# Two empty steps between the transfer of the roots and the products with it, and steps that begin with chunk 0 in the first layer

## The chip, the cores and the metric

The kernel runs on one core of a Trainium2 chip. The metric is the device time of one execution in microseconds (us); the number for a kernel is the median of several runs. The profile comes from one more execution with the hardware profiler on.

## What is computed

Causal block attention over 4 batches of 8 heads, then two feed-forward layers over the 2304 tokens. The first layer multiplies two products; the second normalises its input by the root of the mean square, gates with a sigmoid and multiplies. Cut to what matters here:

```python
x = attention(q, k, v)                 # (2304, 512), blocks of 64 masked causally
a, b = x @ w_a, x @ w_b                # d_model 512, d_ff 1536
x = (a * b) @ w_out                    # the first layer's output
rms = np.sqrt(np.mean(x * x, axis=-1, keepdims=True) + 1e-06)
xn = x / rms * rms_g                   # the step that is edited
g = xn @ w_gate
val = xn @ w_val
out = (g * (1 / (1 + np.exp(-g))) * val) @ w_out2
```

## The kernel before, in words

The tokens run along the free dimension, so an activation tile has 128 partitions of features and up to 768 columns of tokens. Every matrix product is made of three matmuls, with operands split into a high and a low part (names that begin with h and l; `split` at L99 and L109 makes them, the high part on ScalarE).

The first layer runs over five blocks of tokens (512, 256, 512, 512, 512), the second over three blocks of 768, each in two halves of 384. A block goes through d_ff in chunks: 12 chunks in the first layer (`moe1`), 24 in the second (`moe2`), where a chunk is half of the work for one of the two weight matrices over a pair of d_ff tiles. Between chunks lie the output products (`output`, L438 to L440), whose sums VectorE adds into `acc` (L447). Attention and the preparation of the weights for the second layer run beside the first layer.

In the second layer a product by blocks needs seven matrix products per weight matrix. Their sums are formed on VectorE out of PSUM: `u` (L528) from a copy p of the first product and the second, then `p` (L539) and a second `u` (L545), then c (L547, L550, L554), then the gate: `asb` (L561) or `g` (L566), and the split hh, hl of g. TensorE has six PSUM banks for this, so a bank is free for the next product only when VectorE has read it.

Normalisation of the next block is done while the current block is worked on. `normed` is a generator: each `next` runs it to its next `yield`, which is called a step here. Its steps are: squares of the four feature groups and their sum on ScalarE and VectorE (L688 to L691) and the split of the sum into sh and sl (steps 1 and 2); the sum over partitions on TensorE with a matrix of ones (L702, L703, tile r), and a transfer of the row of means to DRAM (step 3); a transfer that spreads it over 128 partitions of 6 numbers (step 4); the root and its reciprocal on 128 x 6 numbers and a transfer back (L710 to L716, step 5); and the transfer that spreads the row of roots over all partitions, into y (L718, step 6). Then come four products of x with the weights of the norm and y (L722, one per step), four differences T of halves of x (L642, one per step), and one step that hands them over. For the first block of the second layer seven more steps split these operands; for later blocks that is done with the last output products.

The steps are called in `before_fc`, before each chunk: two per chunk in the last block of the first layer (of 12 chunks), one per chunk in the second layer (of 24 chunks), from chunk 1 on in both.

```python
            if fc >= 1:
                for _ in range(FC * 2 // n_tiles):
                    got["x"] = next(norm, None) or got.get("x")
```

Which instruction stands where on an engine is not the program's order alone: a scheduler places the instructions of each engine by their priority, which follows the place where they are emitted, and by its own estimate of when their inputs are ready. `behind(ins, "gate")` adds that an instruction stands behind the latest g. All transfers are issued on SyncE's queue, in order: weights (L230, L234, L238), blocks of weights to be prepared (L162), outputs, and the small rows of the steps.

Of the kernel before, what the change touches and what calls it, by code (L numbers as in the profile page):

```python
# [45 lines left out]
def tile_attention_moe_moe(  # L46
# [57 lines left out]
    def split(hi, lo, src, eng_hi, eng_lo, late=None):  # L104

        ins = copy(eng_hi, hi, src)
        if eng_hi is act and late is not None:
            behind(ins, late)
        eng_lo.tensor_tensor(lo, src, hi.bitcast(F32), ALU.subtract)  # L109
        return ins  # L110
# [5 lines left out]
    def behind(ins, what):  # L116

        if what in gate:
            tc.add_manual_dep(ins.ins, gate[what].ins.name, ORDER, reason="keep behind")
# [116 lines left out]
    def fetch_o(layer, i):  # L236
        t = wtiles["o", i] = wop.tile([P, 2, TF * DM], F32R, tag="o", name="o")
        sp.dma_start(out=t.bitcast(F32), in_=wo_dram[layer][i])  # L238
# [392 lines left out]
    def sums_of(x):  # L631


        n = x.shape[2] // 2
        b = {f"B{k + 1}{m + 1}": x[:, 2 * k:2 * k + 2, m * n:m * n + n] for k in range(2) for m in range(2)}
        for e, name, p, q, tag in (
            (dve, "T1", "B12", "B11", "sq"), (dve, "T3", "B22", "B12", "t"),
            (dve, "T2", "B22", "T1", "y"), (dve, "T4", "T2", "B21", "sl"),
        ):
            t = rms["sb"].tile([P, 2 * n], F32, tag=tag, name=name)  # L640
            b[name] = t.rearrange("p (c n) -> p c n", c=2)
            behind(e.tensor_tensor(b[name], b[p], b[q], ALU.subtract), "gate")  # L642
            yield None
        yield b

    def split_sums(b, res):

        for name, el in (
            ("B11", dve), ("T2", dve), ("B21", dve), ("T1", dve), ("T3", pool), ("B22", dve), ("T4", pool),
        ):  # L650
            res[name] = [rms["sb"].tile(list(b[name].shape), F32R, tag=k + name, name=k + name) for k in "hl"]
            split(*res[name], b[name], act, el, "hh")
            yield None
# [27 lines left out]
    def normed(t0, n, parts):  # L681

        xr, ps_r = rms["sb"], rms["ps"]
        x = xr.tile([P, KC, BMAX[1]], F32, tag="xf", name="xf")[:, :, 0:n]
        sp.dma_start(out=x, in_=x2_dram[:, :, t0:t0 + n])
        sq = xr.tile([P, BMAX[1]], F32, tag="sq", name="sq")[:, 0:n]
        y = xr.tile([P, BMAX[1]], F32, tag="y", name="y")[:, 0:n]
        behind(act.activation(sq, x[:, 0, :], AF.Square), "hh")  # L688
        for c in range(1, KC):
            act.activation(y, x[:, c, :], AF.Square)  # L690
            dve.tensor_tensor(sq, sq, y, ALU.add)  # L691
            if c == 2:
                yield None
        sh = xr.tile([P, BMAX[1]], F32R, tag="sh", name="sh")[:, 0:n]
        sl = xr.tile([P, BMAX[1]], F32R, tag="sl", name="sl")[:, 0:n]
        split(sh, sl, sq, act, dve, "hh")
        yield None

        row, small = dram.tile([2, n], F32, name="row"), xr.tile([P, 3, n // P], F32, tag="sm", name="sm")
        for o, w in parts:  # L700
            ps = ps_r.tile([P, 512], F32, tag="r", name="r")
            pe.matmul(ps[:, 0:w], rms["ones"], sh[:, o:o + w], start=True, stop=False)  # L702
            pe.matmul(ps[:, 0:w], rms["ones"], sl[:, o:o + w], start=False, stop=True)  # L703
            dve.tensor_scalar(sq[0:1, o:o + w], ps[0:1, 0:w], 1.0 / DM, 1e-6, ALU.mult, ALU.add)
        sp.dma_start(out=row[0:1, :], in_=sq[0:1, :])
        v, r, t = (small[:, x, :] for x in range(3))
        yield None
        behind(sp.dma_start(out=v, in_=row[0, :].rearrange("(p n) -> p n", p=P)), "gate")
        yield None
        behind(act.activation(r, v, AF.Sqrt), "hh")  # L710
        dve.reciprocal(r, r)
        dve.tensor_tensor(t, r, r, ALU.mult)
        dve.tensor_tensor(t, t, v, ALU.mult)
        dve.tensor_scalar(t, t, -0.5, 1.5, ALU.mult, ALU.add)
        dve.tensor_tensor(r, r, t, ALU.mult)
        sp.dma_start(out=row[1, :].rearrange("(p n) -> p n", p=P), in_=r)  # L716
        yield None
        behind(sp.dma_start(out=y, in_=row[1, :].partition_broadcast(P)), "gate")  # L718
        yield None
        for c in range(KC):  # L720
            behind(
                dve.scalar_tensor_tensor(x[:, c, :], x[:, c, :], rms_g[:, c:c + 1], y, ALU.mult, ALU.mult),  # L722
                "gate",
            )
            yield None
        for b in sums_of(x):
            yield b
        if t0 == blocks[NB_FIRST][1]:

            res = {}  # L730
            for _ in split_sums(b, res):
                yield res
# [4 lines left out]
    for at, (layer, t0, n_tok, parts) in enumerate(blocks):  # L737
        following = blocks[at + 1] if at + 1 < len(blocks) else None
        with_attention = at + 1 < NB
        if layer == 1 and blocks[at - 1][0] == 0:  # L740
# [4 lines left out]
            accs = ctx.enter_context(tc.tile_pool(name="acc2", bufs=1))  # L745
        acc = accs.tile([P, KC, BMAX[layer]], F32, tag="acc", name="acc")
        norm = normed(*following[1:]) if following and following[0] == 1 else iter(())
        got = {}

# [7 lines left out]
        def before_fc(fc, n_tiles=n_tiles, at=at, layer=layer, following=following, norm=norm, got=got):  # L757
            if at == 0:
                if fc > 0:
                    for _ in range(TF):  # L760
                        if prepared[0] < len(w_pieces) // 2:
                            prepare()
            else:
                if layer == 1 and fc in (0, 4, 12, 20):
                    fetch_o(layer, (0, 4, 12, 20).index(fc))
                if layer == 0 and fc % TF == 0:
                    fetch_o(layer, fc // TF)
                if layer == 1 and rings and fc == 0 and blocks[at - 1][0] == 0:
                    for i in range(2, 6):
                        fetch_ab(layer, i)  # L770
                ahead = 2 if layer == 0 else 6
                if fc + ahead < n_tiles:
                    fetch_ab(layer, fc + ahead)
                if layer == 0:
                    n = sum(BACKGROUND[:at]) + min(BACKGROUND[at], BACKGROUND[at] * (fc + 1) // (FC - 3))
                    while prepared[0] < len(w_pieces) // 2 + n:
                        prepare()
            ahead = 2 if layer == 0 else 6
            if following and fc + ahead >= n_tiles:
                fetch_ab(following[0], fc + ahead - n_tiles)  # L780
            if fc >= 1:
                for _ in range(FC * 2 // n_tiles):
                    got["x"] = next(norm, None) or got.get("x")

# [99 lines left out]
```

## Time and profile before

| | |
|---|---|
| median of 3 runs | 1134.62 us (1134.28 to 1134.89) |
| profiled execution, its own time | 1126.49 us |
| its span, first to last instruction | 1124.7 us |
| TensorE (PE) busy | 1076.7 us, 96% |
| VectorE (DVE) busy | 748.1 us, 67% |
| ScalarE (ACT) busy | 523.6 us, 47% |
| GpSimd (POOL) busy | 466.9 us, 42% |
| mean granted TensorE clock | 0.989 |

A time is read against the profiled execution when it comes from the trace. An engine's busy share tells how much of the span it worked; what a wait costs is read where TensorE stands still.

### The profile page before, as it was taken

To read this page: it belongs to the slowest core of one execution; us is meant where nothing else is said; L and a number is where in the kernel's file an instruction comes from. 1 tells how busy PE (TensorE), PEld (TensorE's weight loads), DVE (VectorE), ACT (ScalarE), POOL (GpSimd) and SP (SyncE) were. 2 spreads that over 40 slices of the span, in tenths; PEclk is the share of its full clock that TensorE was granted. 3 is DMA by queue.
4 is the path that set the end of the run, shared out by engine and by line. 5 is a ranking of instruction groups with operands and counts; after the bars stand their busy time and mean duration, and the time that the engine had idled before them with its cause. 6 is when DMAs were issued, how large, how long until landed. Compare 5 with 4: busy or idle time off the path is not lost.

```text
span 1124.7 us, 16248 instructions
## 1 busy us (share of the span) xinstructions
PE 1076.7 (96%) x5780; PEld 956.7 (85%) x5780; DVE 748.1 (67%) x1379; ACT 523.6 (47%) x1142; POOL 466.9 (42%) x460
## 2 busy tenths in 40 slices
PE   6889989999999999899999999989999899999998
PEld 4667768689888788688887878989999899999998
DVE  5988887856876867534547483775677746765564
ACT  6877876746666765424433433431233322223120
POOL 5676677543555765335535443311222211222120
PEclk9999999999999999999999999999999999999999
DMA  5544877877887867969987889845757556475521
GB/s 176 187 155 146 276 249 253 269 268 274 296 301 260 265 245 281 327 238 374 351 316 275 315 328 379 330 165 187 253 213 281 204 187 242 175 267 196 190 82 57
DMA packets 74279, 276.48 MB, mean 246 GB/s; under 512 B 25683, under 2 KB 33363, under 8 KB 56278
## 3 DMA queue, kind: packets, MB, share of 16 engines
q1 hardware_dynamic: 74198, 275.44, 68.7%
q8 instruction: 46, 0.75, 0.3%
q14 instruction: 35, 0.29, 0.1%
HBM read 218.77 MB, written 56.64 MB: 245 GB/s over the span
## 4 chain that ended last, share of the span: by engine, by line
PE 66%; DMA 11%; DVE 10%; POOL 5%; ACT 4%; issue 3%; SPq 0%; POOLq 0%; ACTq 0%; DVEq 0%
PE mm L438 7%; PE mm L439 7%; PE mm L440 7%; PE mm L506 6%; PE mm L508 6%; PE mm L507 6%; PE mm L476 6%; PE mm L478 6%; PE mm L477 6%; PE s L312 3%; DMA st<-in_w_ab_dram 3%; DMA st<-in_w_o_dram 2%; DMA ab<-wc 2%; PE t L373 2%; PE t L347 2%
## 5 line engine op out<-in xcount | busy, mean ns | idle before, releaser
L438 PE MATMUL mm<-hh,o 128*128 128x384 f32 (+2 forms) x528 | 189.7, 363 | 8.0 <-DVE u L528 3.8
L439 PE MATMUL mm<-hh,o 128*128 128x384 f32 (+2 forms) x528 | 187.9, 357 | 0.0
L476 PE MATMUL mm<-xh,ab 128*128 128x512 f32 (+1 forms) x480 | 181.8, 382 | 2.5 <-DVE acc L447 1.1
L477 PE MATMUL mm<-xl,ab 128*128 128x512 f32 (+1 forms) x480 | 181.7, 379 | 0.0
L440 PE MATMUL mm<-hl,o 128*128 128x384 f32 (+2 forms) x528 | 181.1, 355 | 0.0
L478 PE MATMUL mm<-xh,ab 128*128 128x512 f32 (+1 forms) x480 | 180.1, 376 | 0.0
L109 POOL TENSOR_TENSOR hl<-g,hh 128x384 fp32r<-128x384 f32 (+2 forms) x76 | 87.1, 1146 | 157.9 <-ACT hh L99 156.9
L99 ACT ACTIVATE hh<-g 128x384 fp32r<-128x384 f32 (+2 forms) x132 | 70.7, 552 | 143.2 <-DVE g L566 84.1
L561 POOL TENSOR_TENSOR asb<-c,sig 128x384 f32<-128x384 f32 x36 | 37.4, 1038 | 222.4 <-ACT sig L559 222.4
L336 POOL TENSOR_SCALAR pp<-pp,st 128x64 f32<-128x64 f32 (+3 forms) x144 | 87.6, 624 | 76.9 <-DVE st L333 45.3
L438 PEld LDWEIGHTS mm<-hh,o 128*128 128x128 f32 x528 | 100.4, 190 | 19.9 <-DVE u L528 4.1
L312 PE MATMUL s<-ks,qz 128*128 128x384 f32 (+4 forms) x284 | 97.9, 434 | 11.2 <-ACT pp L321 11.0
L439 PEld LDWEIGHTS mm<-hh,o 128*128 128x128 f32 x528 | 100.6, 191 | 8.8 <-issue 1.6
L476 PEld LDWEIGHTS mm<-xh,ab 128*128 128x128 f32 x480 | 91.0, 190 | 19.6 <-DVE acc L447 1.7
L440 PEld LDWEIGHTS mm<-hl,o 128*128 128x128 f32 x528 | 99.9, 190 | 8.6 <-DVE hl L109 0.5
L447 DVE SCALAR_TENSOR_TENSOR acc<-mm,acc 128x384 f32<-128x384 f32 (+2 forms) x132 | 74.3, 587 | 46.7 <-PE mm L440 46.0
L477 PEld LDWEIGHTS mm<-xl,ab 128*128 128x128 f32 x480 | 90.7, 189 | 16.3 <-issue 0.7
L478 PEld LDWEIGHTS mm<-xh,ab 128*128 128x128 f32 x480 | 90.6, 189 | 16.3 <-issue 0.7
L506 PE MATMUL mm<-hT,ab 128*128 128x384 f32 x288 | 97.1, 338 | 2.8 <-DVE u L528 1.9
L507 PE MATMUL mm<-lT,ab 128*128 128x384 f32 x288 | 97.0, 337 | 0.0
L508 PE MATMUL mm<-hT,ab 128*128 128x384 f32 x288 | 95.0, 337 | 0.0
L321 ACT ACTIVATE pp<-s,st 128x288 f32<-128x288 f32 (+8 forms) x142 | 71.4, 505 | 40.3 <-DVE st L315 36.9
(128 smaller groups left out, 2342.3 us busy)
## 6 DMA issues: line engine op xcount, KB each, us to landing
ab<-wab SPq DMA_DIRECT2D x48, 1024.0 KB, 7.0
o<-wo SPq DMA_DIRECT2D x28, 1536.0 KB, 7.4
ab<-wc SPq DMA_DIRECT2D x36, 1024.0 KB, 7.3
ab<-wc SPq DMA_DIRECT2D x36, 768.0 KB, 4.5
st<-in_w_ab_dram SPq DMA_DIRECT2D x48, 512.0 KB, 4.1
wc<-bg SPq DMA_DIRECT2D x12, 1792.0 KB, 7.1
wab<-ab SPq DMA_DIRECT2D x12, 1024.0 KB, 5.1
st<-in_w_o_dram SPq DMA_DIRECT2D x24, 512.0 KB, 4.5
```

Source lines behind the costliest of these rows:

```text
L109: eng_lo.tensor_tensor(lo, src, hi.bitcast(F32), ALU.subtract)
L312: pe.matmul(ps[:, 0:z - a], qz[m % 2][:, b], ks[m][:, a:z], start=True, stop=True)
L336: pool.tensor_scalar(t, t, s[:, 10 + y:11 + y], 1.0, ALU.mult, ALU.mult)
L438: pe.matmul(ps[:, 0:n], wh, hh, start=(y == 0), stop=False)
L439: pe.matmul(ps[:, 0:n], wl, hh, start=False, stop=False)
L440: pe.matmul(ps[:, 0:n], wh, hl, start=False, stop=(y == TF - 1))
L476: pe.matmul(ps[:, 0:n], wh[:, a:z], xhc, start=(c == 0), stop=False)
L477: pe.matmul(ps[:, 0:n], wh[:, a:z], xlc, start=False, stop=False)
L478: pe.matmul(ps[:, 0:n], wl[:, a:z], xhc, start=False, stop=(c == KC - 1))
L506: pe.matmul(ps[:, 0:n], wh, xh[:, c, :], start=(c == 0), stop=False)
L507: pe.matmul(ps[:, 0:n], wh, xl[:, c, :], start=False, stop=False)
L508: pe.matmul(ps[:, 0:n], wl, xh[:, c, :], start=False, stop=(c == 1))
```

## The change

The transfer of the roots keeps its step 6. Two empty steps, 7 and 8, come behind it, so that the four products are steps 9 to 12 and not 7 to 10, and all later steps come two later. In the first layer the steps begin with chunk 0 instead of chunk 1 (`layer` is 0 there): steps 1 to 6 come one chunk earlier, the products come in chunks 4 and 5 as before, and 24 steps are called where 22 were. In the second layer the steps still begin with chunk 1, steps 1 to 6 stay, and products and differences come two chunks later.

```diff
@@ -716,7 +716,8 @@
         sp.dma_start(out=row[1, :].rearrange("(p n) -> p n", p=P), in_=r)
         yield None
         behind(sp.dma_start(out=y, in_=row[1, :].partition_broadcast(P)), "gate")
-        yield None
+        for _ in range(3):
+            yield None
         for c in range(KC):
             behind(
                 dve.scalar_tensor_tensor(x[:, c, :], x[:, c, :], rms_g[:, c:c + 1], y, ALU.mult, ALU.mult),
@@ -778,7 +779,7 @@
             ahead = 2 if layer == 0 else 6
             if following and fc + ahead >= n_tiles:
                 fetch_ab(following[0], fc + ahead - n_tiles)
-            if fc >= 1:
+            if fc >= layer:
                 for _ in range(FC * 2 // n_tiles):
                     got["x"] = next(norm, None) or got.get("x")
```

No instruction is added or removed. Three places in the order of the engines follow. A number behind a name is a buffer's; it differs between the two programs for the same thing. The products are at L722 before and at L723 after, one line lower.

VectorE in the second layer's first block, before (xf are the products, u, p and c the sums out of PSUM, asb and g the gate, T a difference):

```order
L561 TENSOR_TENSOR asb_7459<-c_7433,sig 128x384
L722 SCALAR_TENSOR_TENSOR xf<-xf,rms_g,y 128x768 x4
L528 TENSOR_TENSOR u_7488<-p_7479,mm 128x384
L642 TENSOR_TENSOR T_7507<-xf 128x768
L566 SCALAR_TENSOR_TENSOR g<-mm,asb_7455 128x384
L539 TENSOR_TENSOR p_7503<-u_7488,mm 128x384
L545 TENSOR_TENSOR u_7516<-u_7488,mm 128x384
```

and now:

```order
L561 TENSOR_TENSOR asb_7457<-c_7431,sig 128x384
L723 SCALAR_TENSOR_TENSOR xf<-xf,rms_g,y 128x768 x2
L528 TENSOR_TENSOR u_7486<-p_7477,mm 128x384
L723 SCALAR_TENSOR_TENSOR xf<-xf,rms_g,y 128x768
L539 TENSOR_TENSOR p_7501<-u_7486,mm 128x384
L545 TENSOR_TENSOR u_7513<-u_7486,mm 128x384
L566 SCALAR_TENSOR_TENSOR g<-mm,asb_7453 128x384
```

The first product still follows the same asb; two of the four products now stand behind the first u, the fourth further back behind the g's, and T with it.

VectorE in the second layer's second block, before:

```order
L566 SCALAR_TENSOR_TENSOR g<-c_8797,asb_8739 128x384
L722 SCALAR_TENSOR_TENSOR xf<-xf,rms_g,y 128x768
L109 TENSOR_TENSOR hl<-g,hh 128x384
L566 SCALAR_TENSOR_TENSOR g<-c_8806,asb_8743 128x384
L566 SCALAR_TENSOR_TENSOR g<-c_8815,asb_8747 128x384
L722 SCALAR_TENSOR_TENSOR xf<-xf,rms_g,y 128x768 x3
L528 TENSOR_TENSOR u_8856<-p_8847,mm 128x384
L109 TENSOR_TENSOR hl<-g,hh 128x384
L642 TENSOR_TENSOR T_8959<-xf 128x768
L539 TENSOR_TENSOR p_8871<-u_8856,mm 128x384
L545 TENSOR_TENSOR u_8883<-u_8856,mm 128x384
```

and now:

```order
L566 SCALAR_TENSOR_TENSOR g<-c_8796,asb_8739 128x384
L109 TENSOR_TENSOR hl<-g,hh 128x384
L566 SCALAR_TENSOR_TENSOR g<-c_8805,asb_8743 128x384
L566 SCALAR_TENSOR_TENSOR g<-c_8814,asb_8747 128x384
L723 SCALAR_TENSOR_TENSOR xf<-xf,rms_g,y 128x768 x3
L109 TENSOR_TENSOR hl<-g,hh 128x384
L528 TENSOR_TENSOR u_8854<-p_8845,mm 128x384
L539 TENSOR_TENSOR p_8869<-u_8854,mm 128x384
L545 TENSOR_TENSOR u_8881<-u_8854,mm 128x384
```

The first product left its place in front of hl and two g; three products stand behind these, the fourth and T behind the next chunk's g.

TensorE in the first layer's last block, before (r is the sum over partitions of sh and sl; L438 to L440 are the output products of the first three chunks):

```order
L438 MATMUL mm<-hh,o 128x512
L439 MATMUL mm<-hh,o 128x512
L440 MATMUL mm<-hl,o 128x512 x2
L702 MATMUL r<-sh,ones_r 128x384 x2
L440 MATMUL mm<-hl,o 128x512 x2
L438 MATMUL mm<-hh,o 128x512
L703 MATMUL r<-sl,ones_r 128x384 x2
```

and now (L476 to L478 are the products of the second chunk; 36 matmuls of the block lie ahead of the first r):

```order
L476 MATMUL mm<-xh,ab 128x512
L477 MATMUL mm<-xl,ab 128x512
L478 MATMUL mm<-xh,ab 128x512
L702 MATMUL r<-sh,ones_r 128x384 x2
L476 MATMUL mm<-xh,ab 128x512
L477 MATMUL mm<-xl,ab 128x512
L478 MATMUL mm<-xh,ab 128x512
L703 MATMUL r<-sl,ones_r 128x384 x2
```

The sum over partitions moved from the first output products to the middle of the second chunk. On ScalarE the squares and the split sh moved with it: the block's first decoding step `a` (L137) stood in front of the squares and now stands between them and sh. On SyncE's queue the four small transfers of the steps (L705, L708, L716, L718) moved ahead by about one weight load each in this block; in the second layer they stand where they stood.

## Rows read from the trace of the kernel before

**Rows 1.** The page, part 1: busy time, share of the span and instructions of each engine.

```profile
PE 1076.7 (96%) x5780; PEld 956.7 (85%) x5780; DVE 748.1 (67%) x1379; ACT 523.6 (47%) x1142; POOL 466.9 (42%) x460
```

**Rows 2.** Waits of TensorE, 560 to 1125 us: waited for, total us, times, longest.

```profile
PE mm L438 <- DVE u L528: 3.8, 1, 3.8
PE mm L506 <- DVE u L528: 1.9, 1, 1.9
PE mm L506 <- DVE u L545: 0.9, 1, 0.9
PE mm L506 <- DMA ab<-wc: 0.8, 1, 0.8
PE mm L476 <- DVE acc L447: 0.7, 1, 0.7
PE mm L438 <- ACT hh L99: 0.4, 1, 0.4
```

**Rows 3.** Chain that ended last, 735 to 752 us: start, us, what.

```profile
735.45 5.53 DMA y<-row
...
746.35 0.32 PE mm L438
...
750.64 0.17 PE mm L439
```

**Rows 4.** VectorE in order, second layer's first block: start, us, what, idle before.

```profile
741.00 3.98 DVE L722 SCALAR_TENSOR_TENSOR xf<-xf,rms_g,y 128x768 f32<-128x768 f32 x4 [2.99 <-DMA y<-row]
744.91 0.54 DVE L528 TENSOR_TENSOR u<-p,mm 128x384 f32<-128x384 f32 x1
745.38 0.94 DVE L642 TENSOR_TENSOR T<-xf 128x768 f32<-128x768 f32 x1
```

**Rows 5.** The same view of VectorE, second layer's second block.

```profile
873.49 1.02 DVE L722 SCALAR_TENSOR_TENSOR xf<-xf,rms_g,y 128x768 f32<-128x768 f32 x1 [1.25 <-DMA y<-row]
874.43 0.55 DVE L109 TENSOR_TENSOR hl<-g,hh 128x384 fp32r<-128x384 f32 x1
...
875.83 3.64 DVE L722 SCALAR_TENSOR_TENSOR xf<-xf,rms_g,y 128x768 f32<-128x768 f32 x3
879.39 0.54 DVE L528 TENSOR_TENSOR u<-p,mm 128x384 f32<-128x384 f32 x1
```

**Rows 6.** The same view of VectorE, first layer's last block.

```profile
647.45 3.80 DVE L722 SCALAR_TENSOR_TENSOR xf<-xf,rms_g,y 128x768 f32<-128x768 f32 x4 [3.18 <-DMA y<-row]
```

**Rows 7.** Stretches: length, busy us of each engine (instructions), granted clock, DMA, GB/s.

```profile
746.20:749.50 3.30, 3.30 (x12) 3.30 (x11) 3.30 (x8) 1.01 (x2) 1.01 (x1) 0.50 0.27 112
882.70:886.00 3.30, 3.30 (x12) 3.30 (x12) 1.91 (x4) 0.52 (x1) 0.00 (x0) 0.50 0.30 127
298.40:300.10 1.70, 0.00 (x0) 0.00 (x0) 1.63 (x4) 0.46 (x1) 1.30 (x3) 1.00 0.90 333
300.20:303.70 3.50, 3.15 (x25) 2.96 (x26) 1.96 (x7) 0.91 (x5) 0.56 (x1) 1.00 1.13 247
164.50:166.20 1.70, 0.00 (x0) 0.00 (x0) 1.46 (x3) 1.32 (x4) 0.29 (x1) 0.90 1.21 199
166.00:172.60 6.60, 6.33 (x15) 4.96 (x16) 6.43 (x15) 4.28 (x12) 4.05 (x4) 0.50 0.93 328
```

**Rows 8.** The roots' transfer, line L718, three times: from issue to landing.

```profile
DMA to landing us min/median/max: 3.6/5.5/7.4
```

**Rows 9.** ScalarE and TensorE in order, start of the first layer's last block.

```profile
599.63 0.67 ACT L137 ACTIVATE a<-st 128x512 f32<-128x512 f32 x1 [9.34 <-DMA st<-in_w_o_dram]
...
594.67 0.39 PE L476 MATMUL mm<-xh,ab 128*128 128x512 f32 x1
...
602.83 0.39 PE L476 MATMUL mm<-xh,ab 128*128 128x512 f32 x1
```

**Rows 10.** The page, part 6: weight loads of the first layer, KB, us to landing.

```profile
ab<-wab SPq DMA_DIRECT2D x48, 1024.0 KB, 7.0
```

**Rows 11.** Transfers of weights to be prepared, line L162: from issue to landing.

```profile
DMA to landing us min/median/max: 3.3/4.2/9.0
```

## The prediction

> **What bounds the kernel now.** I read the page first: TensorE is busy for 96% of the span [rows 1], so the time is TensorE's time, and only three things can move it: its amount of work, the stops in which it stands still, and the stretches in which its clock is halved. The diff adds no work to it. The second view is the list of what TensorE waited for from 560 us on, where both edited places lie [rows 2]. That list is short: 8.5 us in six stops of 0.4 us or more, and three of them, 3.8, 1.9 and 0.9 us, end with a VectorE addition of the second layer (u, lines 528 and 545). The other three are 0.8 (a weight transfer), 0.7 (VectorE's accumulation, L447) and 0.4 us.
>
> Why is u late? The chain and VectorE's own order of time show it. In the second layer's first block the transfer that spreads the row of roots takes 5.53 us [rows 3]. VectorE stands 2.99 us for it, then does the four products of L722 in a row in 3.98 us, and only then u, at 744.91 [rows 4]. TensorE has by then run out of free PSUM banks. That is the 3.8 us stop. In the next block VectorE waits 1.25 us, does one product, three short instructions, then three products from 875.83, and u starts at 879.39 [rows 5]: the stops of 1.9 and 0.9. In the first layer's last block the wait is 3.18 us [rows 6], and the accumulations queued behind the products come late: the stop of 0.7.
>
> The third view is the granted clock. After each of the two places one stretch runs at 0.50, that is 1.2 GHz instead of 2.4: in 3.30 us TensorE starts 12 matmuls there [rows 7]. The chain gives the price: one matmul per 0.32 us against 0.17 [rows 3]. About 11 matmuls fall into such a stretch, so it costs 11 x 0.15 = 1.6 us.
>
> **The second layer's first block.** The transfers stand where they stood in SyncE's queue, so I let the row land at the same 741.0. What the changed order moves are the products: two of the four now stand behind u, one of them between u and the next addition p, where the difference T (0.94 us in [rows 4]) stood before, and the fourth behind the gating products g. u comes two products earlier, 3.98 / 2 = 2.0 us, and the stop shrinks from 3.8 to 1.8 us. The order from u to p keeps its length, one operation of about 1 us in between, so I expect no new stop behind it (at most 0.4 us, since p, u and g come in another order). The differences T are late next; they are needed only at the block's end, and cost nothing as long as VectorE has the output products of TensorE to hide behind.
>
> Does the clock still fall? The trace has two stops of nearly this length, both with TensorE at 0.00 busy over 1.7 us: after the one at 164.5 the clock is 0.50, after the one at 298.4 it stays at 1.00 [rows 7]. That is even; I take the fall to stay, since the stop has the length of one that was followed by it. Gain here: 2.0 us, with 3.6 as the other end.
>
> **The second layer's second block.** Here all four products are moved behind a short VectorE chain that used to stand behind the first product. Before: wait to 873.49, one product, then hl and two g (874.43 to 875.83, 1.4 us), three products (3.64 us), u at 879.39. After: hl and the two g run inside the wait, which began at 873.49 - 1.25 = 872.24; with about 0.6 us for ScalarE's hh ahead of them (hl of the same shape takes 0.55) they end near 872.2 + 0.6 + 1.4 = 874.2. The row is there by then, so VectorE waits for nothing; three products of the same 3.64 us end near 877.9, one more hl (0.5) follows, and u starts at 878.4, so 1.0 us earlier. The stop of 1.9 becomes 0.9. Behind u no T of 0.94 us stands any more: p and the second u follow directly, 0.9 us earlier still, while TensorE has six matmuls to do (6 x 0.17 = 1.0 us). That removes the stop of 0.9. Together 2.8 becomes 0.9: gain 1.9. Stops of 0.7 and 0.8 us in [rows 2] lie in stretches that kept their clock, so I take this fall to vanish: 1.6 more, 3.5 in all. Its ends: if the row takes as long as the slowest of the three (7.4 against 3.6 us in [rows 8]), it lands at 877.3, 3 us after VectorE asks, the stop is 3.8 instead of 2.8 and the clock falls: a loss of 1.0.
>
> Against counting a clock gain while a stop remains stands one rule. The rows first: the stops of 0.7 and 0.8 us were followed by no fall. The Trainium skill, "TensorE: Matmul & The Clock Gate", section "A second HAM failure mode: psum-queue depth-cycling", says that short idles between groups of matmuls, from cycling through PSUM banks, are enough to make the clock go back and forth. By that rule the 0.9 us stop would still cost the fall, and the sum would be 1.6 us smaller; the rows on the two shorter stops speak against it here.
>
> **The first layer's last block.** The first six steps come one chunk earlier (two steps per chunk), two are empty, and the products keep chunk 4. The row of roots is therefore issued about one chunk earlier, and a chunk is 24 matmuls. 36 of them take from the block's start at 594.67 to 602.83 [rows 9], so a chunk is 5.4 us: more than the 3.18 us that VectorE waited. The wait goes, the products no longer delay L447, and the 0.7 us stop goes. The stop of 0.4 waits for ScalarE, on which the early steps' squares lie; these move too, so it may go or come back elsewhere. I count 0.7, between 0 and 1.1. On SyncE's queue four small transfers of these steps are now ahead of weight loads. Each may hold the queue until its source is ready, which costs nothing while the weights come in time: they are fetched two chunks ahead, 10.8 us, land in 7.0 us [rows 10], and no stop in [rows 2] names them. Without that cover each us of delay is a us of stop.
>
> **The sum.** 2.0 + 3.5 + 0.7 = 6.2 us. The profiled execution took 1126.49 us, and would take 1120.3. The median of the runs is 8.1 us above it; I carry the difference over unchanged: 1134.62 - 6.2 = 1128.4 us.
>
> **The rivals.**
> - *The clock stays up at both places*: the first block's 1.8 us stop behaves like the one at 298.4, and 6.2 + 1.6 = 7.8 us go: 1126.8. The two rows are even, but it also needs the second block's fall to vanish. 0.25.
> - *The clock falls at both places*: the banks are still full when u comes in the second block, TensorE idles 0.9 us, and some 11 matmuls after it run at 0.32 us each. 6.2 - 1.6 = 4.6 us, 1130.0. Against it stand the two shorter stops without a fall. 0.12. (The rule of "TensorE: Matmul & The Clock Gate" in the Trainium skill, above, would give this one.)
> - *The wait is the row, not the place*: in the second block the row lands as late as the slowest. 2.0 - 1.0 + 0.7 = 1.7 us, 1132.9. The three landings differ by a factor of two [rows 8], so it can be. 0.08.
> - *The change hardly does what it says*: the empty steps move no wait, since the scheduler, not the step, places the products, and in the first block it still puts the first one where VectorE stood 2.99 us. If the second block's products were bound the same way, 2.0 us would be all: 1132.6. The new order there speaks against it. 0.09.
> - *Slower*: in the first layer the two sum products on TensorE (r, L702 and L703) now stand in the first two chunks, and TensorE executes in order. Their operand sh stands on ScalarE behind a decoding step a that waited 9.34 us for a weight transfer, until 599.63 [rows 9]. From there 0.67 us for a and about 0.94 us each for sh and sl (an estimate, from T of the same 768 columns in [rows 4]) give 602.2; TensorE asks for sh at 602.83 and for sl about 1 us later, 603.9. So there is 1.7 us of room. Past that each us stops TensorE, with a fall of the clock on top. With the slowest such transfer, 9.0 against 4.2 us median [rows 11], 4.8 us longer: a stop of 3.1 plus 1.6 leaves 0.8 of the 5.5 us of the other layer. It turns slower by over 0.2% from a landing about 8 us later: 1134.62 - 5.5 + 6.3 + 1.6 = 1137.0. No transfer in the trace was that late. 0.06.
>
> **How the numbers follow.** The forecast itself has 0.40. About 0.2% (2.3 us) is what a measurement of this kernel can tell from no change. Forecast and the first two rivals are faster by more than that: 0.40 + 0.25 + 0.12 = 0.77. The third and fourth, 1.7 and 2.0 us, are within it: 0.17. The last is slower: 0.06. The range goes from 1125.7, which is the best case with the first layer's other 0.4 us and some tenths of spread between runs (0.6 us in the three shown), to 1133.0, which takes in both cases within 0.2%; it leaves out the slower case and the tails, under 0.2.
>
> **What would show it.** Right: TensorE's stop for u in the second layer's first block near 1.8 us, in the second below 1; one half-clock stretch from 700 us on, not two; no wait for the row in the first layer and 1 us or less in the second block, still about 3 us in the first; T behind the next g. Wrong: a wait of VectorE for the row as long as before in the second block; a stop of TensorE at r in the first layer; a stop with a weight load as its end; or stops that shrink as said while the time stays, which would mean that TensorE's pace, and not its stops, sets the end.

## The result, and the profile after

| | before | after |
|---|---|---|
| median | 1134.45 us (1132.15 to 1134.89, 4 runs) | 1119.42 us (1117.65 to 1121.29, 4 runs) |
| ratio after to before | | 0.9878, 95% interval 0.9856 to 0.9901 |
| profiled execution | 1126.49 us | 1118.77 us |
| mean granted clock | 0.989 | 0.992 |

The change makes the kernel faster by 1.2%, 15.0 us in these runs, where 6.2 were forecast. The sign was right; the time lies 6.3 us under the range.

The page of the kernel after, part 1, against [rows 1]: VectorE, ScalarE and GpSimd do the same work, and TensorE's 5780 matmuls take 4.8 us less.

```profile
PE 1071.9 (96%) x5780; PEld 954.7 (85%) x5780; DVE 750.6 (67%) x1379; ACT 523.3 (47%) x1142; POOL 465.6 (42%) x460
```

The waits of TensorE in the kernel after, 560 to 1125 us (the view of [rows 2]: waited for, total us, times, longest). Of the six stops two are left. All three of the first layer and of the border between the layers are gone, of which the prediction had counted one.

```profile
PE mm L438 <- DVE u L528: 2.0, 1, 2.0
PE mm L506 <- DVE u L528: 1.2, 1, 1.2
```

VectorE in order in the kernel after (the view of [rows 4 to 6]: start, us, what, idle before). First the first layer's last block, then the second layer's first block, then its second block.

```profile
633.91 6.53 DVE L723 SCALAR_TENSOR_TENSOR xf<-xf,rms_g,y 128x768 f32<-128x768 f32 x4
...
738.26 2.37 DVE L723 SCALAR_TENSOR_TENSOR xf<-xf,rms_g,y 128x768 f32<-128x768 f32 x2 [2.74 <-DMA y<-row]
740.56 0.54 DVE L528 TENSOR_TENSOR u<-p,mm 128x384 f32<-128x384 f32 x1
741.03 1.00 DVE L723 SCALAR_TENSOR_TENSOR xf<-xf,rms_g,y 128x768 f32<-128x768 f32 x1
741.96 0.54 DVE L539 TENSOR_TENSOR p<-u,mm 128x384 f32<-128x384 f32 x1
...
869.88 0.55 DVE L566 SCALAR_TENSOR_TENSOR g<-c,asb 128x384 f32<-128x384 f32 x1
870.35 3.64 DVE L723 SCALAR_TENSOR_TENSOR xf<-xf,rms_g,y 128x768 f32<-128x768 f32 x3
873.91 0.54 DVE L109 TENSOR_TENSOR hl<-g,hh 128x384 fp32r<-128x384 f32 x1
874.37 0.54 DVE L528 TENSOR_TENSOR u<-p,mm 128x384 f32<-128x384 f32 x1
```

Only the first block still waits for the row of roots (2.74 us against 2.99), and u comes behind two products and not four. In the second block there is no wait for the row any more: the products start right behind g, and u stands behind three products and one hl. In the first layer the products run at 633.91 where they ran at 647.45 [rows 6], with no wait.

Stretches of the kernel after (the view of [rows 7]: length, busy us of PE, PEld, DVE, ACT and POOL, granted clock, DMA share, GB/s). One short stretch at 1.2 GHz is left behind 700 us; from there to the end the clock stays at 2.4 GHz.

```profile
741.80:745.10 3.30, 3.30 (x12) 3.30 (x11) 3.30 (x8) 0.98 (x2) 1.01 (x1) 0.50 0.80 328
745.10:1116.00 370.90, 367.28 (x2116) 366.51 (x2114) 236.29 (x411) 102.98 (x198) 73.51 (x65) 1.00 0.54 192
```

### The profile page after: what moved, and what is told of

Its sections match the earlier page's. It is cut to its first block, busy times and chain, and to the rows that moved or that the text cites. A ratio compares the mean times of both kernels' runs of the same rounds, so it can differ in the third digit from the quotient of the medians.

```text
span 1116.9 us, 16248 instructions
## 1 busy us (share of the span) xinstructions
PE 1071.9 (96%) x5780; PEld 954.7 (85%) x5780; DVE 750.6 (67%) x1379; ACT 523.3 (47%) x1142; POOL 465.6 (42%) x460
## 4 chain that ended last, share of the span: by engine, by line
PE 70%; DVE 9%; DMA 7%; ACT 5%; POOL 5%; issue 3%; SPq 0%; POOLq 0%; ACTq 0%; DVEq 0%
PE mm L438 8%; PE mm L439 7%; PE mm L440 7%; PE mm L476 7%; PE mm L477 7%; PE mm L478 7%; PE mm L506 6%; PE mm L507 6%; PE mm L508 6%; DMA st<-in_w_ab_dram 4%; PE s L312 3%; PE t L373 2%; POOL x L140 2%; PE t L347 2%; POOL pp L336 1%
## 5 line engine op out<-in xcount | busy, mean ns | idle before, releaser
L438 PE MATMUL mm<-hh,o 128*128 128x384 f32 (+2 forms) x528 | 189.6, 363 | 6.3 <-DVE acc L447 2.1
L476 PE MATMUL mm<-xh,ab 128*128 128x512 f32 (+1 forms) x480 | 180.7, 379 | 1.7 <-DVE xh L101 1.0
L440 PE MATMUL mm<-hl,o 128*128 128x384 f32 (+2 forms) x528 | 180.4, 355 | 0.0
L478 PE MATMUL mm<-xh,ab 128*128 128x512 f32 (+1 forms) x480 | 179.9, 375 | 0.0
L438 PEld LDWEIGHTS mm<-hh,o 128*128 128x128 f32 x528 | 100.5, 191 | 17.9 <-DVE acc L447 3.5
L440 PEld LDWEIGHTS mm<-hl,o 128*128 128x128 f32 x528 | 100.0, 190 | 8.4 <-issue 0.5
L476 PEld LDWEIGHTS mm<-xh,ab 128*128 128x128 f32 x480 | 90.5, 189 | 18.2 <-DVE xh L101 1.4
L478 PEld LDWEIGHTS mm<-xh,ab 128*128 128x128 f32 x480 | 90.4, 188 | 16.2 <-issue 0.7
L447 DVE SCALAR_TENSOR_TENSOR acc<-mm,acc 128x384 f32<-128x384 f32 (+2 forms) x132 | 73.9, 587 | 42.4 <-PE mm L440 41.9
```

Of the source, the lines that this page charges most:

```text
L438: pe.matmul(ps[:, 0:n], wh, hh, start=(y == 0), stop=False)
L440: pe.matmul(ps[:, 0:n], wh, hl, start=False, stop=(y == TF - 1))
L476: pe.matmul(ps[:, 0:n], wh[:, a:z], xhc, start=(c == 0), stop=False)
L478: pe.matmul(ps[:, 0:n], wl[:, a:z], xhc, start=False, stop=(c == KC - 1))
```

## The experiments

Every kernel here has the same 5780 matmuls on TensorE. So besides the lists of waits, the start of the nth matmul can be compared between executions. I cut each trace at the 2900th matmul (before the last block of the first layer, near 581 us) and at the 3560th (in the second layer, ahead of the first edited place, near 725 us). Ahead of the first cut lie attention and the first layer's other blocks, where every kernel here has the same order of instructions; I call this stretch attention. The table in "Where the prediction was right and wrong" is made of these cuts, and of the stretches from the 3560th to the 3800th and from the 4300th to the 4550th matmul, which hold the two edited places of the second layer.

### Each half alone, and both kernels again

The second-layer half alone: the kernel after, with the first layer as before (`blocks[NB_FIRST]` is the second layer's first block, so the condition holds for the steps that run in the first layer).

```diff
-        for _ in range(3):
+        for _ in range(1 if t0 == blocks[NB_FIRST][1] else 3):
...
-            if fc >= layer:
+            if fc >= 1:
```

> Only the second layer gets the two empty steps; the first layer's last block keeps steps from chunk 1 and its products at step 7. From the two traces the second layer's part is 1.9 us in its first block and 3.4 in its second, 5.3 us. Theory A: about 5 us faster than before, between 4 and 6.5, and the stops at r, acc and the first-layer weight transfer stay. Rival (the first layer's part is what matters, because it moves the whole weight preparation): under 2 us faster.

Measured: 1124.09 us (1121.49 to 1127.23, 6 runs), ratio 0.9937 (0.9914 to 0.9959) against 1130.61 us for the kernel before on the same chip.

The first-layer half alone: the kernel after, without empty steps in the second layer.

```diff
-        for _ in range(3):
+        for _ in range(3 if t0 == blocks[NB_FIRST][1] else 1):
```

> Only the first layer's last block is changed: steps from chunk 0, two empty steps ahead of its products; the second layer's steps are as before. From the two traces this part is 3.7 us (0.1 + 1.1 at the sums, 1.0 at the accumulation, 0.5 at the next output products, 1.1 at the weight transfer at the layers' border). Theory A: about 3.7 us faster than before, between 2.5 and 5. Rival (the border's weight transfer and the small stops are chance, and only the 0.7 us stop goes): about 1 us faster.

Measured: 1125.11 us (1122.27 to 1126.61, 6 runs), ratio 0.9942 (0.9919 to 0.9965).

The kernel after, unchanged, in the same comparison:

> The changed kernel again, beside its two halves on the same chip. Theory A: the gains of the halves add, 9 us, as in the two traces. Rival (the runs' 15 us are real on one chip): 13 to 15 us faster, and then the sum of the two halves either reaches that, or falls short of it because they help each other.

Measured: 1118.61 us (1116.13 to 1122.81, 6 runs), ratio 0.9890 (0.9866 to 0.9913).

And the kernel before, unchanged, as one of the runs:

> The kernel before, unchanged, for a second trace of it. Theory A (the stops of the first trace are the whole story, and its 1126.5 us is as usual a time as the 1134.5 us of the runs): time as the runs shown, 1132 to 1135 us, and a trace with the same three stops at u and acc (3.8, 1.9 + 0.9, 0.7 us) and two half-clock stretches behind 700 us, whatever its span. Theory B (the 8 us between that trace and the runs are further stops of the same kind, which the first trace happened not to have): a trace near 1134 us whose TensorE stops behind 560 us sum to about 17 us and not 9, at the row of roots or at weight loads. Theory C (the 8 us lie elsewhere, in attention, ahead of the edited places): the matmul that begins at 560 us in the first trace begins some 6 to 8 us later.

Measured: 1130.51 us (1126.81 to 1136.63, 12 runs), ratio 1.0003 (0.9985 to 1.0022).

So the second-layer half gives 6.5 us, the first-layer half 5.5, both together 12.0: the halves add, within intervals of some 2.5 us to either side. For the second layer 5.5 were forecast, for the first 0.7. The kernel before spreads over 10 us here.

The waits of TensorE with the first-layer half alone, 560 to 1125 us: what is left is the second layer's stops of the kernel before; the first layer's and the border's are gone.

```profile
PE mm L438 <- DVE u L528: 3.8, 1, 3.8
PE mm L506 <- DVE u L528: 3.1, 1, 3.1
PE mm L506 <- DVE u L545: 0.6, 1, 0.6
```

The same view with the second-layer half alone: the first layer's stops stand, and the weight transfer (ab<-wc) at the border with them.

```profile
PE mm L506 <- DVE u L528: 2.1, 1, 2.1
PE mm L438 <- DVE u L528: 2.0, 1, 2.0
PE mm L506 <- DMA ab<-wc: 1.5, 1, 1.5
PE mm L476 <- DVE acc L447: 0.7, 1, 0.7
PE r L703 <- DVE sl L109: 0.2, 1, 0.2
```

In this execution neither second-layer stop was followed by a lower clock; here is the stretch between the two.

```profile
745.00:876.00 131.00, 131.00 (x754) 130.62 (x754) 92.63 (x158) 42.43 (x78) 28.45 (x24) 1.00 0.62 223
```

The waits of TensorE in this second trace of the kernel before (an execution of 1136.63 us), same view, against [rows 2]: the stops of the second layer are 9.2 us in sum where they were 6.6.

```profile
PE mm L438 <- DVE u L528: 4.2, 1, 4.2
PE mm L506 <- DVE u L528: 4.0, 1, 4.0
PE mm L506 <- DMA ab<-wc: 1.4, 1, 1.4
PE mm L506 <- DVE u L545: 1.0, 1, 1.0
```

Its second block on VectorE, against [rows 5]: the wait for the row is 3.36 us and not 1.25.

```profile
882.54 1.02 DVE L722 SCALAR_TENSOR_TENSOR xf<-xf,rms_g,y 128x768 f32<-128x768 f32 x1 [3.36 <-DMA y<-row]
...
884.88 3.61 DVE L722 SCALAR_TENSOR_TENSOR xf<-xf,rms_g,y 128x768 f32<-128x768 f32 x3
888.41 0.54 DVE L528 TENSOR_TENSOR u<-p,mm 128x384 f32<-128x384 f32 x1
```

And its stretches at 1.2 GHz, against [rows 7]: each is twice as long.

```profile
750.40:757.10 6.70, 5.83 (x18) 5.84 (x19) 5.41 (x11) 1.02 (x2) 1.01 (x1) 0.50 0.43 178
...
890.30:897.00 6.70, 5.74 (x19) 5.73 (x19) 3.89 (x8) 1.42 (x3) 0.44 (x1) 0.50 0.13 55
```

What follows: one trace of the kernel before doesn't tell how long these stops are. None of the three theories fits as stated. Of the 10.1 us by which this execution is longer than the one of the prediction, 4.7 lie in attention, 0.4 in the first layer's last block and border, and 4.7 in the second layer.

### Is a short stop or a long one usual?

The kernel before twice more, for its trace.

> The kernel before a third time, for its trace. Theory (the wait for the row differs from execution to execution, and the one that the prediction was made on had a short one): the stops of the second layer's second block add to 3.5 to 5.0 us, as in four of the five traces with this order, against 2.8 in the one that the prediction used; the second layer takes 397 to 400 us from the 3560th matmul on. Rival (2.8 us is what is usual): 2.5 to 3.2 us, 395 to 396 us.

Measured: 1130.51 us; stops of the second block 2.2 + 1.0 = 3.2 us, 395.9 us from the 3560th matmul on. The rival's numbers.

> The kernel before a fourth time, for its trace; as for the third: by the theory the stops of the second block add to 3.5 to 5.0 us and the second layer takes 397 to 400 us, by the rival 2.5 to 3.2 us and 395 to 396 us.

Measured: 1131.52 us; 4.6 + 0.5 = 5.2 us (5.16 unrounded), 399.0 us. The stop lies just above the theory's upper end of 5.0, the stretch within it. Neither is "usual": the stop varies. What sets it can be read in SyncE's queue. The transfer of the roots (L718) first waits there until the row, written to DRAM by L716, has landed; then it takes its own time to land. SyncE's wait at L718 in this trace, second block (view of SyncE's waits, 850 to 895 us), and VectorE's product there:

```profile
SPq L718 <- DMA row<-sm: 7.0, 1, 7.0
```

```profile
877.67 1.02 DVE L722 SCALAR_TENSOR_TENSOR xf<-xf,rms_g,y 128x768 f32<-128x768 f32 x1 [4.00 <-DMA y<-row]
```

Nine traces have the order of before in the second layer (four of the kernel before, five of first-layer variants, four of them in the next section). In order of the sum of SyncE's wait at L718 and the landing of y:

| trace | wait + landing, us | TensorE's stops in the second block, us | half clock behind them, us |
|---|---|---|---|
| before, the one of the prediction | 4.9 + 3.6 = 8.5 | 2.8 | 3.4 |
| chunk 0 alone, third | 4.8 + 3.9 = 8.7 | 3.0 | none |
| before, third | 5.1 + 3.9 = 9.0 | 3.2 | none |
| first-layer half | 4.5 + 5.0 = 9.5 | 3.6 | 6.8 |
| chunk 0 alone, first | 5.6 + 4.5 = 10.1 | 4.0 | 3.4 |
| before, second | 6.1 + 4.4 = 10.5 | 5.0 | 6.8 |
| empty steps alone | 6.4 + 4.4 = 10.8 | 4.6 | 6.8 |
| chunk 0 alone, second | 6.6 + 4.5 = 11.1 | 4.6 | 3.4 |
| before, fourth | 7.0 + 4.7 = 11.7 | 5.2 | 6.8 |
| after, second trace | 5.0 + 3.5 = 8.5 | 1.2 | none |
| after | 5.8 + 4.4 = 10.2 | 1.2 | none |
| second-layer half | 6.4 + 4.6 = 11.0 | 2.1 | none |

In the order of before 3.2 us more of transfer go with 2.3 us more of stop. In this block the prediction's trace had the fastest transfers of the nine and the shortest stop. With two empty steps the stop is 1.2 us until the transfers take some 10 us, and only the slowest of the three shows in it.

### Which part of the first-layer half gives the 5.5 us?

The kernel before, with steps that begin with chunk 0 and no empty steps:

```diff
-            if fc >= 1:
+            if fc >= layer:
```

> Kernel before with the steps beginning with chunk 0 in the first layer, and no empty step anywhere: in the first layer's last block everything, transfer of the roots and products alike, comes one chunk earlier; the second layer is that of the kernel before. The whole first-layer half of the change (both parts) gave 5.5 us (1125.1 against 1130.6). Theory A (VectorE's wait for the row of roots, with the four products in one piece behind it, makes the accumulations and the later work late): transfer and products keep their distance, so VectorE still waits some 3 us for the row, one chunk earlier, and the gain is 0 to 1 us: 1129.5 to 1130.6. Theory B (the order of the transfers on SyncE's queue, and the earlier end of the steps, free the border between the layers): the gain is most of the 5.5 us, 1125 to 1127, and the weight-transfer stop at the layers' border is gone.

Measured: 1126.97 us (1124.32 to 1133.74, 12 runs), ratio 0.9974 (0.9957 to 0.9992), against 1129.97 us. Its trace, an execution of 1133.74 us, did not show where 3 us were gained, so it ran twice more.

> The kernel whose steps begin with chunk 0 in the first layer, without empty steps, a second time: its time was 3.0 us below the kernel before, but its one trace shows the first layer's last block 0.8 us longer than before (145.6 us from TensorE's 2900th to its 3560th matmul, against 144.5 to 145.0) and the second layer 397.3 us (395.4 to 400.2 in the traces with this order). Theory (neither part alone frees the first layer, since without the empty steps the products still ask before the row has landed): 145 to 146 us again there, and the time is 0 to 2 us below before. Rival (that one trace was an unlucky one, the early row alone is worth most of it): 141 to 143 us there, and the time is again 3 us below.

Measured: 1128.23 us (1122.59 to 1133.66, 10 runs), ratio 0.9993 (0.9970 to 1.0015), against 1129.1 us; 143.0 us between the two cuts.

> The same kernel a third time, for its trace. Theory: the first layer's last block takes 145 to 146 us from the 2900th to the 3560th matmul. Rival: 141 to 143 us.

Measured: 1127.92 us; 144.0 us. The three traces have 145.6, 143.0 and 144.0, mean 144.20, against 144.85 (144.5 to 145.3) for five with the first layer of before. Of the two new traces one has the rival's number (142.99 unrounded), the other neither's; nor do the times agree well with the mean: a gain of 0.7 us by the traces, 0.9 to 3.0 by the two timings. VectorE's wait for the row of 3 us, which theory A expected here too, did not come: it is 0.8, 0 and 0.4 us in the three traces.

The kernel before with the empty steps alone, in the first layer; since two more steps are needed there, its last two chunks call three each.

```diff
-        yield None
+        for _ in range(3 if t0 == blocks[NB_FIRST][1] else 1):
+            yield None
...
-                for _ in range(FC * 2 // n_tiles):
+                for _ in range(FC * 2 // n_tiles + (layer == 0 and fc > 9)):
```

> Kernel before with the two empty steps in the first layer's last block alone, and the steps beginning with chunk 1 as before; since two more steps are needed there, the last two chunks of that block call three steps and not two. The transfer of the roots stays, the products come one chunk (about 5.4 us) later, so VectorE's wait for the row of 3.2 us goes. Theory A: 4 to 5.5 us are gained, 1125 to 1127; the weight-transfer stop at the border stays or goes with chance. Theory B: no gain, 1130 to 1131, and the stop at the border stays; the three steps per chunk at the end may cost up to 1 us.

Measured: 1129.31 us (1124.69 to 1131.83, 12 runs), ratio 0.9989 (0.9972 to 1.0006); 143.7 us between the cuts, 1.2 less than before, in one trace; the interval of its time includes no change. So each part alone is worth about 1 us by the traces, and both together 4.0 (140.8 in five traces, 140.77 to 140.88). Theory A, that the empty steps alone take the wait away, falls with the row of the products in the first layer's last block, which stands where [rows 6] has it:

```profile
646.80 3.81 DVE L723 SCALAR_TENSOR_TENSOR xf<-xf,rms_g,y 128x768 f32<-128x768 f32 x4 [3.11 <-DMA y<-row]
```

The scheduler had put the products later than their step in the kernel before; two more steps don't move them on VectorE. Theory B of chunk 0 alone falls too: there the stop at the border is still there, and others are new. Its first trace's waits of TensorE, 580 to 712 us:

```profile
PE mm L440 <- DVE hl L109: 1.0, 2, 0.8
PE mm L506 <- DMA ab<-wc: 0.9, 1, 0.9
PE mm L438 <- ACT hh L99: 0.6, 2, 0.3
```

Why hl is late is to be seen on VectorE. In the second trace with chunk 0 alone, the products run where they run in the kernel after, but the differences T follow at once, from 641.27 on, the gate that hl is split from is done 3 us later than in the kernel after, and the fourth T comes just behind hl:

```profile
634.22 6.53 DVE L722 SCALAR_TENSOR_TENSOR xf<-xf,rms_g,y 128x768 f32<-128x768 f32 x4
640.67 0.68 DVE L139 SCALAR_TENSOR_TENSOR st<-st 128x512 uint32<-128x512 uint32 x1
641.27 0.94 DVE L642 TENSOR_TENSOR T<-xf 128x768 f32<-128x768 f32 x1
...
646.79 0.68 DVE L109 TENSOR_TENSOR hl<-g,hh 128x512 fp32r<-128x512 f32 x1
647.39 0.95 DVE L642 TENSOR_TENSOR T<-T,xf 128x768 f32<-128x768 f32 x1
```

In the kernel after, the last two T stand at 651.90 and 653.23, behind the accumulations. So the first part takes the early steps and the wait for the row out of the way, and the second keeps what follows the products from being pushed into the gates. The lists of waits divide the stops in the same way. With chunk 0 alone those at L447 and at r are gone in all three traces, and the border's is left, with 0.5 to 0.9 us. With the empty steps alone the border's is gone in the one trace, and L447 (0.6 us) and hh (0.9 us in two stops) are left. That the T's and the later splits are the reason for each of the new stops was not tried by itself, and why the weight transfer at the border comes in time is not shown.

### More empty steps in the second layer

The kernel after with five empty steps in the second layer's blocks, and with seven (8 in place of the 6 below):

```diff
-        for _ in range(3):
+        for _ in range(3 if t0 == blocks[NB_FIRST][1] else 6):
```

> The kernel after with five empty steps and not two in the second layer's blocks (first layer as in the kernel after). In the second layer's first block all four products now stand behind the next u, a whole chunk behind the stop that is left there (2.0 us, with 3.4 us at half clock behind it). Theory (the left stop is the wait for the row, ahead of u): the wait of 2.5 us for the row goes, the stop and the half clock go with it, 2.0 + 1.6 = 3.6 us less than the kernel after: 1115.0. Rival (a row of four products of 1.0 us each is enough to make the next sums late, wait or not): the stop only moves and becomes 1.5 to 2.5 us behind the products, and the time stays within 1 us of 1118.6. Second rival: the differences T are late for the block's end, TensorE waits there, 1120 to 1122.

Measured: 1112.80 us (1111.61 to 1114.30, 4 runs), ratio 0.9853 (0.9831 to 0.9874) against 1129.97 us. This beats both kernels: 17 us under the kernel before. TensorE's list of waits from 560 us on is empty, and the clock never falls there. Stretches of this kernel over the two edited places, TensorE busy for all of both:

```profile
735.00:765.00 30.00, 30.00 (x175) 30.00 (x174) 18.58 (x32) 9.16 (x19) 5.66 (x6) 1.00 0.60 218
...
865.00:895.00 30.00, 30.00 (x175) 30.00 (x174) 18.50 (x31) 10.17 (x21) 5.23 (x5) 1.00 0.58 212
```

Its VectorE in the second block, in order of time:

```profile
878.93 4.55 DVE L723 SCALAR_TENSOR_TENSOR xf<-xf,rms_g,y 128x768 f32<-128x768 f32 x4
883.41 0.54 DVE L109 TENSOR_TENSOR hl<-g,hh 128x384 fp32r<-128x384 f32 x1
890.11 0.56 DVE L528 TENSOR_TENSOR u<-p,mm 128x384 f32<-128x384 f32 x1 [6.16 <-PE mm L508]
```

All four products in a row cost TensorE nothing here, since VectorE then waits 6.16 us for TensorE. In the kernel after, three of them stand just ahead of u, with no wait for the row, and TensorE stops for 1.2 us. So the wait for the row is not all of it: the place within the chunk counts as well. From the 3560th matmul on it takes 384.8 us against 390.2 in the kernel after: 3.8 us of the 5.4 in the first block, where the theory had 3.6, and 1.6 in the second, which it had not counted. The rival, that a row of four products is enough to make the sums late wherever it stands, falls.

> As the one with five empty steps, but seven: the four products are split two and two over two chunks in both blocks, and the last T comes just ahead of the block's last chunks. Theory (wait for the row): same as five, 1115.0. Rival (a row of four products is the cause): only this one gains, by 2 to 3.6 us against the kernel after, 1115.0 to 1116.6, while five empty steps stay near 1118.6. Second rival (T late at the end of the block): slower than five empty steps by 1 us or more.

Measured: 1115.12 us (1113.35 to 1117.07, 5 runs), ratio 0.9873 (0.9852 to 0.9893). TensorE has no stop behind 560 us here either, and the second layer takes 384.9 us as with five empty steps, so no T is late. In the two traces the first matmul to the 2900th, attention, takes 575.8 us here and 574.1 there, at work that none of these edits touches; why the medians differ by 2.3 us is not settled. Attention varies by more than that with the same order of instructions: it takes 574.0 to 579.2 us in the fourteen traces.

## Where the prediction was right and wrong

Mean times from the traces, in us, by the cuts named above:

| place | order of before (traces) | order of after (traces) | gain | forecast |
|---|---|---|---|---|
| first layer's last block and border | 144.8 (5) | 140.8 (5) | 4.0 | 0.7 |
| second layer, first block | 47.9 (9; 47.1 to 48.8) | 45.0 (3; 44.1 to 45.5) | 2.8 | 2.0 |
| second layer, second block | 49.6 (9; 46.9 to 51.9) | 45.2 (3; 44.9 to 45.9) | 4.3 | 3.5 |
| sum | | | 11.2 | 6.2 |

The sum, 11.2 before rounding, is near the 12.0 us of the timed comparison on one chip. By layer the two agree less well: 4.0 against 5.5 us in the first, 7.2 against 6.5 in the second, which the intervals of the timing allow.

**The second layer's first block: right.** The stop went from 3.8 to 2.0 us, 1.8 was the forecast; u comes behind two products, and the wait for the row stands. The clock was called even, and it fell in two of the three traces with this order, behind stops of 1.95 to 1.96 us in all three. The price of a fall was about right: with these stops the block took 45.4 and 45.5 us with a fall of 3.4 us and 44.1 without one, 1.3 us; in the second block with the order of before, less the stops, three traces with a fall of 3.4 us took 45.2 to 45.5 us and the two without one 43.9, so 1.3 to 1.6, where the forecast had 1.6.

**The second layer's second block: the mechanism right, the size taken from the best case.** The wait for the row is gone, the stop behind u L545 is gone and so is the fall of the clock. The stop that is left is 1.2 and not 0.9 us. Against the prediction's own trace both blocks together gave 395.4 - 390.2 = 5.2 us, 5.5 forecast. But that trace had the shortest stop of nine in this block. What the step took as given, when the row lands, was read from the three landings of y alone [rows 8]; in the nine traces these take 3.6 to 5.0 us in this block, the transfer ahead, which L718 waits for, holds it for 4.5 to 7.0 us, and no row of that one was read.

**The step that failed: "I carry the difference over unchanged".** The profiled execution of before lay 8.1 us under the median, and that was read as a constant. It was a fast execution: in the second layer it is 1.9 us under the mean of nine, in the first layer's last block 0.3 under the mean of five, in attention 1.9 under the mean of four traces of the kernel before. The profiled executions of after lie 0.7 us under the first median and 1.8 under the second. Of the 9.0 us by which the forecast was too high, 8.1 - 0.7 = 7.4 lie in this step. 2.2 of them are in the two layers' places, whose stops the change removes, so that this part of the difference shrinks with them. 1.5 are chance: attention, which the change does not touch, took that much longer in the profile of after than in that of before. The rest, some 4 us, stays open: the first runs of before had a median of 1134 us, the later ones, with 13 to 23 runs each, 1129.1 to 1130.6. Counted by places instead, the gain of the table is 5.0 us more than the forecast, 3.3 of them in the first layer, and the open part is the 3.8 us that its 11.2 lack of the 15.0 of the first runs. The spread that the range allowed, 0.6 us from three runs, was too small by the same error: 17 runs span 8.4 us.

**The first layer's last block: the term was mis-sized, 0.7 against 4.0.** Two steps of the argument failed. "The products keep chunk 4" holds for their step and not for VectorE, where they come 13.5 us earlier (14.8 counted from the 2900th matmul) and out of the way of the accumulations. And I counted only the stop at L447 (0.7). The stops for hh (0.4) and for the weight transfer at the border (0.8) went too, as did 0.2 us at r for sl, which the list of waits has beside the six. The stops also cost more than the list says: from the two traces, TensorE's start slips by 0.6 at hh, 0.5 at sl, 0.9 at L447, 0.25 at the next output products and 1.0 at the border, 3.2 us of the 3.7 that this trace loses against the kernel after.

**The rivals.** That the clock stays up at both places came true in one of three executions, with the second-layer half alone. That it falls at both places did not: in the second block no stop of 1.2 us, and not the one of 2.1, was followed by a fall. The Trainium skill, "TensorE: Matmul & The Clock Gate", section "A second HAM failure mode: psum-queue depth-cycling", tells of short idles that come frequently, with each iteration; that one such stop would do was the prediction's reading, and these three stops speak against that reading. *The wait is the row* came only in part, in the second-layer half alone: VectorE waited 0.82 us for the row there, and the gain did not turn into a loss. *The change hardly does what it says* did not come: three products went behind hl and two g, and the wait in front of them is gone in both traces of after. The slower way, r in the first two chunks, did not come: no trace with both parts has a stop at r.

## What to carry to other kernels

Before a gain is sized from one profiled execution, compare that execution with the median: where it lies lower by more than the gain, take more traces, since its stops may not be the typical ones and the difference need not be a constant to be added back. For a wait on a transfer read every transfer in its chain and how each one's landing varies. And look for a place where the engine waits for another one behind the moved work: four products in a row cost nothing ahead of a 6.2 us wait, and three cost 1.2 us ahead of a sum that TensorE needed.

## What the runs showed of the hardware

The clock did not follow the length of a stop alone. Behind stops of 1.95 and 1.96 us it fell to 1.2 GHz in two executions and stayed at 2.4 GHz in one. Behind pairs of 2.8, 3.0 and 3.2 us it fell once and stayed up twice, and behind 3.6 to 5.2 us it always fell, for 3.4 or 6.8 us.

The products took 1.0 us each in some places and up to 2.6 in others. GpSimd in the first layer's last block of the kernel after, in order of time:

```profile
634.74 1.44 POOL L109 TENSOR_TENSOR hl<-g,hh 128x512 fp32r<-128x512 f32 x1 [0.53 <-ACT hh L99]
636.68 2.02 POOL L216 TENSOR_TENSOR bg<-src,bg 128x768 fp32r<-128x768 f32 x1 [0.50 <-ACT bg L213]
```

The second of the four products ran from 634.94 to 636.99 and the third from 636.91 to 639.51: each began 0.2 us after a GpSimd instruction had begun and ended 0.81 us after that instruction's end (636.18 and 638.70), so four of them took 6.5 us where four took 3.8 in the kernel before [rows 6]. The Trainium skill, "SBUF — State Buffer", section "Who interferes with whom", says that a VectorE instruction with two inputs in SBUF contends with a GpSimd instruction that reads SBUF, and that the port pair which they share is an exclusive lock; these two ends agree with it. TensorE's list of waits has no stop there.
